# Issuing the value products of a pair of heads as one alternating group in batch 0 of a fused attention and two-MLP kernel

## The chip, the cores and the metric

The kernel runs on one core of one Trainium2 chip, alone. The metric is the time of one execution on the device, in microseconds (us), the median of several executions. The engines of a core are named as the profile names them: PE (TensorE, matmuls; PEld is its weight loads), DVE (VectorE), ACT (ScalarE), POOL (GpSimd) and SP (the queue that issues most DMAs).

## The reference, cut to what matters

Three stages follow one another: attention, a token-shift MLP with a gate, and a mixer MLP. The change lies in the attention, batch 0.

```python
k_sum = k.reshape(B, H, nb, block, D).max(axis=3)      # B, H, S, D = 2, 8, 768, 64; block 32, nb 24
v_sum = v.reshape(B, H, nb, block, D).mean(axis=3)
scores_l = where(|i - j| < 16, scale * q @ k.T, -1e9)  # a band around the diagonal
scores_s = scale * q @ k_sum.T + log(block)            # the block summaries
a = softmax(concat([scores_l, scores_s]))
x = a @ concat([v, v_sum])                             # -> x: (B, S, H * D)
...
xk = mu_k * x + (1 - mu_k) * x_prev                    # second stage: 512 -> 1024 -> 512
k = relu(xk @ w_k); v = k * k @ w_v; r = sigmoid(xr @ w_r); x = r * v
...                                                    # third stage: token mixing, then 512 -> 1536 -> 512
```

## The kernel before

**Attention.** Each batch has 6 tiles of 128 tokens (t = 0 to 5) and 4 pairs of heads; e = 0 or 1 is the head within a pair. Of one e, the four heads are handled together. For a tile and an e, `s_stage` writes scores (tile sp; 120 columns: 24 block summaries and 96 keys) by 8 matmuls on PE, then for each head one DVE instruction takes mask and minimum (L385, out to pe) and one ACT instruction the exponential with its row sum (L387). `t_stage` transposes the four pe on PE (tile pt) and copies them to SBUF (tile PT, three buffers) on DVE (L410) or ACT (L408). `v_stage` multiplies PT with the values: 8 matmuls of 120x64 by 64 columns for an e, into the lower (e = 0) or upper (e = 1) 64 partitions of tile pv. When both halves of pv are there, batch 0 adds the reciprocal of the row sums: they are turned (L436, L437), spread over partitions by 8 matmuls (tile rb, in one of the two buffers of pt), ACT copies pv to xT (L444), and DVE multiplies by rb (L445). xT is the input of the second stage.

**Steps.** In batch 0 a step is one (t, e): 12 steps, with a filler matmul (spin) in the first eight. In batch 1 a step is a tile with both e: there the 16 value matmuls of a tile are issued as one group that alternates between e = 1 and e = 0, kept in that order by `in_line`; the row sums are applied earlier, on POOL (L399). `LAGS = 1, 2` says how many steps after its scores a tile is transposed and multiplied. In batch 0 before, each e has its own value group of 8.

**Work put in between.** `main()` is the second stage, in chunks of 256 tokens: `mixed` makes xk on POOL (tmp, L533), DVE (xk, L534; xl, L536) and ACT; then for each of four g come 24 matmuls to ko and, one g later, 12 to acc (L544). `attention()` yields costs, and `main()` is advanced by a credit of them. `weights.step()` prepares one of 16 weights of 128x512 in this stage: ACT (L153), two DVE passes (L157, L163, through tile wf with two buffers), a rounding copy on ACT (L174) and the rest on POOL (L175). Chunk 0 goes through all 16. For batch 1, DVE also makes block maxima (ks, L287) and block sums (vrs, L309), and POOL puts the maxima into kw (L293) before its scores can start.

**Order.** A scheduler sets the order of each engine's instructions from program order, given priorities and its own times; after that each engine runs its list in order and waits on semaphores. So a change to when a group is emitted can move instructions on every engine.

Of the kernel before, what the change touches and what calls it, by code (L numbers as in the profile page):

```python
# [23 lines left out]
LAGS = 1, 2  # L24
# [33 lines left out]
def fused_kernel(ctx, tc, q, k, v, vt, mu, w_k, w_v, w_r, w_t1, w_t2, w_c1, w_c2, out):  # L58
# [230 lines left out]
    @ahead(HK)  # L289
    def kw_sums(b, t):  # L290
        st = state[b]
        for o in (0, WC - NB):
            nc.gpsimd.tensor_scalar(st["kw"][t][:, :, o:o + NB], st["ks"], 1.0, 1.0, ALU.mult, ALU.mult)  # L293
# [10 lines left out]
    @ahead(HR)  # L304
    def vt_sum(b, j):
        st = state[b]
        if j == 0:
            st["vr"] = at.tile([128, NP, NB], F32, tag="vrs", bufs=1, name="vrs")
        r = nc.vector.tensor_reduce(st["vr"][:, 2 * j:2 * j + 2], st.pop(("vt", j)), AX.X, ALU.add)  # L309
        if b == 0:  # L310
            behind(r, lows[-1:])

    @ahead(HR)
    def v_gather(b):
        st = state[b]
        vp = bank("pt", 2, [128, NP, 128], "vp")
        for p in range(NP):
            nc.tensor.transpose(vp[:NB, p], st["vr"][:, p], ident)
        st["vs"] = at.tile([NB, DM], F32, tag="vs", bufs=1, name="vs")
        nc.scalar.activation(st["vs"], vp[:NB].rearrange("p g e -> p (g e)"), AF.Copy, scale=1.0 / BLOCK)  # L320

    @ahead(HL)
    def vw_load(b, t):
        ws = []
        for half in range(2):
            w = ybuf[:NC, 2 * t + half] if b == 0 else at.tile([NC, DM], F32, tag="vw", bufs=VB, name="vw")
            row, srow = (NB, 0) if half == 0 else (0, NK)
            key = 128 * t + 64 * half
            after(nc.sync.dma_start(w[row:row + NK], v[b, key:key + NK]))
            ws.append((w, srow))  # L330
        st_of(b)["vw"][t] = ws

    def vw_sums(b, t):
        ahead(HV if b or t == 0 else 0)(copy_sums)(b, t)
# [12 lines left out]
    @ahead(HL)  # L347
    def q_load(b, t):
        if b == 0:
            st_of(b)["qT"][t] = xT[:, :, XB + 1 + 128 * t:XB + 129 + 128 * t]  # L350
        else:
            st_of(b)["qT"][t] = at.tile([128, NP, 128], F32, tag="qT", bufs=QB, name="qT")
        after(nc.sync.dma_start(st_of(b)["qT"][t], q[b, t]))
# [93 lines left out]
    done_tiles = [0]  # L447

    def attention():
        slots = {}  # L450
        n0 = 2 * NT
        steps = [(0, t, (e,)) for t in range(NT) for e in range(2)] + [(b, t, (0, 1)) for b in range(1, B) for t in range(NT)]
        for i in range(len(steps) + 1):
            if i < len(steps):
                b, t, es = steps[i]
                if b and t == 0:
                    yield from prep(b)
                zs = s_stage(b, t, es)
                if len(es) == 1:
                    for what, z, lag in zip((t_stage, v_stage), (zs[0], zs), LAGS):  # L460
                        slots.setdefault(min(i + lag, n0), []).append(((i + lag, lag), what, z))
                else:
                    slots[i + 1] = [((i, 1), n_stage, z) for z in zs] + [((i, 2), t_stage, z) for z in zs] + [((i, 3), v_stage, zs)]
                if i < SPIN_UNITS:
                    spin(SPIN)
                yield 0.95 * len(es)
                if es[-1] == 1 and t + 1 < NT:
                    kw_sums(b, t + 1)
                if b and t == 0:
                    vw_sums(b, 0)  # L470
                if i in VSUM:
                    vt_sum(0, VSUM.index(i))
                if i == VSUM[1]:
                    v_gather(0)
                    vw_sums(0, 0)
            for _, what, z in sorted(slots.get(i, ()), key=lambda s: s[0]):
                what(z)
                if what is t_stage:
                    yield 0.43
                elif what is v_stage:  # L480
                    yield 0.7 * len(z)
                    done_tiles[0] += len(z) / 2
            if i < len(steps):
                if 0 in es:
                    if t + 1 < NT and t + 1 not in state[b]["vw"]:
                        vw_load(b, t + 1)
                    if b and t + 2 < NT:
                        q_load(b, t + 2)
                if i == VSUM[1]:
                    vw_sums(0, 1)  # L490
                elif 1 in es and t + 1 < NT and i > VSUM[1]:
                    vw_sums(b, t + 1)
                if b + 1 < B:
                    for e in es:
                        prep_next(b + 1, 2 * t + e)

    def prep_next(b, j):

        if j >= 4 and j % 2 == 0:
            k_load(b, j // 2 - 2)  # L500
        if j == 9:
            vt_load(b, 0)
            q_load(b, 0)
        if j == 10:
            vt_load(b, 1)
        if j == 2 * NT - 1:
            for t in (4, 5):
                k_load(b, t)
            vw_load(b, 0)
            q_load(b, 1)  # L510

    def prep(b):

        for t in range(NT):
            k_max(b, t)
            yield HOLD / (NT + 2)
        for j in range(2):
            vt_sum(b, j)
            yield HOLD / (NT + 2)
        kw_sums(b, 0)  # L520
        v_gather(b)
# [97 lines left out]
    def spin(n):  # L619

        o = bank("ko", 1, [128, 4, 128], "spin")
        for _ in range(n):
            after(nc.tensor.matmul(o, ident, ident.unsqueeze(1).to_broadcast([128, 4, 128]), start=True, stop=True))
# [50 lines left out]
    for n, cost in enumerate(attention()):  # L674
        weights.pin = PIN0 if n < N0 else PIN1
        if n >= W0 and n % SIDE_EVERY == 0:
            weights.step()
        credit += cost * (RATIO if n < NR else RATIO2)
        while credit > 0:
            got = next(hidden, None)  # L680
            if got is None:
                credit = 0.0
                break
            credit -= got
# [458 lines left out]
```

## Time and profile before

| | |
|---|---|
| time, median of 3 (lowest to highest) | 502.85 us (502.44 to 504.47) |
| span of the profiled execution, first to last instruction | 502.8 us |
| its granted PE clock, mean | 0.990 |
| PE busy | 487.9 us, 97% |
| DVE, ACT, POOL busy | 316.6, 250.9, 217.4 us |

The profile has one execution; its own time is its span, 502.8 us, which equals the median. Times in it are us from its first instruction. Batch 0 of the attention lies between 12 and 75 us. In the rows of a timeline two records of PE belong to one matmul here ("x16" is 8 matmuls).

### The profile page before, as it was taken

To read this page: it belongs to the slowest core of one execution; us is meant where nothing else is said; L and a number is where in the kernel's file an instruction comes from. 1 tells how busy PE (TensorE), PEld (TensorE's weight loads), DVE (VectorE), ACT (ScalarE), POOL (GpSimd) and SP (SyncE) were. 2 spreads that over 40 slices of the span, in tenths; PEclk is the share of its full clock that TensorE was granted. 3 is DMA by queue.
4 is the path that set the end of the run, shared out by engine and by line. 5 is a ranking of instruction groups with operands and counts; after the bars stand their busy time and mean duration, and the time that the engine had idled before them with its cause. 6 is when DMAs were issued, how large, how long until landed. Compare 5 with 4: busy or idle time off the path is not lost.

```text
span 502.8 us, 8800 instructions
## 1 busy us (share of the span) xinstructions
PE 487.9 (97%) x3278; PEld 407.1 (81%) x3278; DVE 316.6 (63%) x638; ACT 250.9 (50%) x569; POOL 217.4 (43%) x266
## 2 busy tenths in 40 slices
PE   7999997999999999999999998999999999999996
PEld 3567785888888888888888887878898999989995
DVE  2888998641514355598889789646579638354352
ACT  1778746862544555686585455454554435111110
POOL 6335587862441447345516434774942813000000
PEclk9899998899999999999999999999999999999999
DMA  8999930221000650000551998639351405253102
GB/s 264 323 309 361 335 87 14 88 80 40 20 1 2 224 196 0 1 0 14 161 163 21 400 394 313 211 112 316 117 168 42 142 31 164 52 200 117 52 1 83
DMA packets 35914, 70.63 MB, mean 140 GB/s; under 512 B 3072, under 2 KB 12288, under 8 KB 35872
## 3 DMA queue, kind: packets, MB, share of 16 engines
q1 hardware_dynamic: 34288, 69.09, 42.0%
q10 hardware_dynamic: 1584, 0.98, 0.7%
q8 instruction: 26, 0.43, 0.3%
q14 instruction: 16, 0.13, 0.1%
HBM read 60.04 MB, written 9.44 MB: 138 GB/s over the span
## 4 chain that ended last, share of the span: by engine, by line
PE 75%; DMA 10%; DVE 8%; POOL 2%; ACT 2%; issue 1%; SPq 1%; DVEq 0%; POOLq 0%
PE ko L544 13%; PE acc L544 13%; PE o L955 12%; PE m L544 11%; PE o L983 7%; PE ro L544 7%; PE go L544 5%; DMA wst<-in_moe_w_k_dram 3%; DMA xT<-in_q_dram 3%; DMA ybuf<-in_v_dram 2%; DVE wf L163 2%; PE pv L425 2%; PE sp L367 2%; PE h L544 2%; DMA wst<-in_moe_w_ch_dram 1%
## 5 line engine op out<-in xcount | busy, mean ns | idle before, releaser
L175 POOL TENSOR_TENSOR w<-wf,w 128x512 fp32r<-128x512 f32 x50 | 69.1, 1387 | 77.3 <-ACT w L174 72.4
L544 PE MATMUL ko<-xh,w 128*128 128x256 f32 x384 | 76.3, 288 | 1.7 <-POOL w L175 0.9
L544 PE MATMUL m<-u,w 128*128 128x256 f32 x504 | 65.1, 283 | 0.8 <-DVE mw L846 0.7
L544 PEld LDWEIGHTS m<-u,w 128*128 128x128 f32 x504 | 63.4, 191 | 2.9 <-DVE mw L846 0.9
L544 PEld LDWEIGHTS ko<-xh,w 128*128 128x128 f32 x384 | 61.1, 188 | 5.4 <-POOL w L175 1.1
L544 PE MATMUL acc<-w,kh 128*128 128x512 f32 x192 | 61.7, 404 | 0.0
L955 PE MATMUL o<-w,gh 128*128 128x512 f32 x192 | 59.1, 391 | 0.0
L544 PE MATMUL ko<-xl,w 128*128 128x256 f32 x192 | 54.4, 283 | 1.1 <-DVE xl L536 1.1
L559 POOL TENSOR_TENSOR kl<-rl,kh 128x512 fp32r<-128x512 f32 x24 | 33.7, 1405 | 44.6 <-ACT kh L558 36.4
L163 DVE SCALAR_TENSOR_TENSOR wf<-wst,wf 128x512 int32<-128x512 int32 x50 | 47.6, 956 | 8.2 <-ACT wst L153 7.1
L174 ACT CAST w<-wf 128x512 fp32r<-128x512 f32 x50 | 30.9, 620 | 42.8 <-DVE wf L163 40.9
L557 DVE TENSOR_TENSOR rl<-rl 128x512 f32<-128x512 f32 x24 | 19.6, 819 | 48.4 <-ACT rl L556 48.2
L387 ACT ACTIVATE pe<-pe,mn 128x120 f32<-128x120 f32 x96 | 36.6, 383 | 14.6 <-DVE mn L385 14.3
L153 ACT ACTIVATE wst<-wst 128x512 f32<-128x512 f32 x62 | 41.1, 675 | 2.1 <-DMA wst<-in_moe_w_ch_dram 2.1
L544 PEld LDWEIGHTS acc<-w,kh 128*128 128x128 f32 x192 | 35.3, 192 | 7.3 <-ACT pe L387 0.3
L955 PEld LDWEIGHTS o<-w,gh 128*128 128x128 f32 x192 | 34.7, 188 | 6.2
L534 DVE SCALAR_TENSOR_TENSOR xk<-xT,mus,tmp 128x256 f32<-128x256 f32 x52 | 36.5, 733 | 4.1 <-POOL tmp L533 3.2
L544 PEld LDWEIGHTS ko<-xl,w 128*128 128x128 f32 x192 | 36.2, 188 | 2.1 <-DVE xl L536 1.3
L544 PE MATMUL acc<-w,kl 128*128 128x512 f32 x96 | 37.7, 403 | 0.0
L955 PE MATMUL o<-w,gl 128*128 128x512 f32 x96 | 37.1, 391 | 0.0
L544 PE MATMUL go<-u,w 128*128 128x512 f32 x144 | 35.6, 393 | 0.0
L784 ACT ACTIVATE gh<-m 128x512 fp32r<-128x512 f32 x24 | 14.2, 596 | 42.7 <-DVE m L846 42.7
(120 smaller groups left out, 964.5 us busy)
## 6 DMA issues: line engine op xcount, KB each, us to landing
wst<-in_moe_w_ch_dram SPq DMA_DIRECT2D x36, 512.0 KB, 6.9
w<-stored SPq DMA_DIRECT2D x24, 512.0 KB, 4.9
stored<-w SPq DMA_DIRECT2D x24, 256.0 KB, 4.7
wst<-in_moe_w_k_dram SPq DMA_DIRECT2D x8, 512.0 KB, 7.4
wst<-in_moe_w_v_dram SPq DMA_DIRECT2D x8, 512.0 KB, 9.5
wst<-in_moe_w_tok_dram SPq DMA_DIRECT2D x6, 512.0 KB, 4.7
out_dram<-o SPq DMA_DIRECT2D x12, 256.0 KB, 2.4
kw<-in_k_dram SPq DMA_DIRECT2D x9, 320.0 KB, 5.1
```

Source lines behind the costliest of these rows:

```text
L153: a = nc.scalar.activation(top.bitcast(F32), top.bitcast(F32), AF.Prelu, scale=2.0 ** -112, alpha=2.0 ** 32)
L163: nc.vector.scalar_tensor_tensor(wi, top, 3, wi, ALU.logical_shift_left, ALU.bitwise_or)
L174: r = nc.scalar.copy(hi, src)
L175: eng.tensor_tensor(lo, src, hi.bitcast(F32), ALU.subtract)
L387: nc.scalar.activation(pe, pe, AF.Exp, bias=mn[:, p:p + 1], scale=-1.0, accum_out=den[:, p:p + 1])
L534: nc.vector.scalar_tensor_tensor(xk[:, d], xT[:, d, x0:x0 + MW], mu[:, d:d + 1], tmp, ALU.mult, ALU.add)
L544: nc.tensor.matmul(o, l, r, start=(first and i == 0), stop=(last and i == 3 * n - 1))
L557: nc.vector.tensor_tensor(rl, rl, rl, ALU.mult)
L559: nc.gpsimd.tensor_tensor(lo, rl, hi.bitcast(F32), ALU.subtract)
L784: nc.scalar.activation(hi, o, AF.Relu)
L955: nc.tensor.matmul(accs[c][t], l, r, start=(first and j == 0 and i == 0), stop=(last and j == 1 and i == 2))
L983: nc.tensor.matmul(accs[0][t], l, r, start=(k == 0 and i == 0), stop=(k == NF2 - 1 and i == 2))
```

## The change

`v_stage` is called once a tile in batch 0, at the lag of e = 1, with both heads of each pair, and so issues its 16 matmuls in the alternating order of batch 1. The transposes stay where they were, one e at a time.

```diff
     def attention():
-        slots = {}
+        slots, pair = {}, []
         n0 = 2 * NT
...
                 zs = s_stage(b, t, es)
                 if len(es) == 1:
-                    for what, z, lag in zip((t_stage, v_stage), (zs[0], zs), LAGS):
-                        slots.setdefault(min(i + lag, n0), []).append(((i + lag, lag), what, z))
+                    pair.extend(zs)
+                    slots.setdefault(min(i + LAGS[0], n0), []).append(((i + LAGS[0], LAGS[0]), t_stage, zs[0]))
+                    if es[0] == 1:
+                        slots.setdefault(min(i + LAGS[1], n0), []).append(((i + LAGS[1], LAGS[1]), v_stage, list(pair)))
+                        pair.clear()
                 else:
```

Lines behind the change have a number higher by 3 in the changed program (L544 is L547 there).

On PE, tile 3 of batch 0. Before, from the scores sp_1000 (tile 4) to the normalisation rb_873: PT_689 is e = 0, PT_776 e = 1.

```order
L367 MATMUL sp_1000<-kw_107,xT_84 64x120 x8
L425 MATMUL pv_781<-PT_689,ybuf_71 64x64 x8
L405 MATMUL pt_850<-ident_61,pe_737 120x128
L405 MATMUL pt_850<-ident_61,pe_740 120x128
L405 MATMUL pt_850<-ident_61,pe_743 120x128
L405 MATMUL pt_850<-ident_61,pe_746 120x128
L425 MATMUL pv_781<-PT_776,ybuf_71 64x64 x8
L441 MATMUL rb_873<-ident_61,dens_521 64x128 x8
```

The same place in the changed program, up to the third of the 16 value matmuls (the next 13 go on alternating, and rb_864 follows them); PT_671 is e = 0, PT_776 e = 1.

```order
L367 MATMUL sp_968<-kw_107,xT_84 64x120 x3
L405 MATMUL pt_810<-ident_61,pe_737 120x128
L405 MATMUL pt_810<-ident_61,pe_740 120x128
L405 MATMUL pt_810<-ident_61,pe_743 120x128
L405 MATMUL pt_810<-ident_61,pe_746 120x128
L425 MATMUL pv_845<-PT_776,ybuf_71 64x64
L425 MATMUL pv_845<-PT_671,ybuf_71 64x64
L425 MATMUL pv_845<-PT_776,ybuf_71 64x64
```

The transposes no longer stand between the two halves; they are ahead of all 16, and the first value matmul now needs the PT of e = 1.

On DVE, from the block sums (vrs) of the second half of batch 1 to the first masking of batch 1's tile 0 (L385, printed as ISA). Before:

```order
L309 TENSOR_REDUCE vrs<-ybuf 128x48
L163 SCALAR_TENSOR_TENSOR wf<-wst,wf 128x512
L157 TENSOR_SCALAR wf<-wst 128x512
L163 SCALAR_TENSOR_TENSOR wf<-wst,wf 128x512
L445 TENSOR_TENSOR xT<-xT,rb 128x4x128
L157 TENSOR_SCALAR wf<-wst 128x512
L534 SCALAR_TENSOR_TENSOR xk<-xT,mus,tmp 128x256
L163 SCALAR_TENSOR_TENSOR wf<-wst,wf 128x512
L534 SCALAR_TENSOR_TENSOR xk<-xT,mus,tmp 128x256
L557 TENSOR_TENSOR rl<-rl 128x512
L157 TENSOR_SCALAR wf<-wst 128x512
L385 ISA pe,mn<-sp,mask_182 128x120
```

In the changed program:

```order
L309 TENSOR_REDUCE vrs<-ybuf 128x48
L560 TENSOR_TENSOR rl<-rl 128x512
L410 COPY PT<-pt 120x512
L163 SCALAR_TENSOR_TENSOR wf<-wst,wf 128x512
L157 TENSOR_SCALAR wf<-wst 128x512
L385 ISA pe,mn<-sp,mask_182 128x120
L385 ISA mn 128x1
```

The first L163 in each is that of the twelfth weight. The masking of batch 1 has moved up to directly behind it, and the last xT of batch 0 and the xk that come from it have moved behind the masking.

On DVE, from the first xl to the copy of PT for tile 4, e = 1. Before:

```order
L536 TENSOR_TENSOR xl<-xk,xh 128x1024
L437 RECIPROCAL dens<-dens 128x8
L157 TENSOR_SCALAR wf<-wst 128x512
L445 TENSOR_TENSOR xT<-xT,rb 128x4x128
L410 COPY PT<-pt 120x512
```

In the changed program:

```order
L539 TENSOR_TENSOR xl<-xk,xh 128x1024
L163 SCALAR_TENSOR_TENSOR wf<-wst,wf 128x512
L157 TENSOR_SCALAR wf<-wst 128x512
L163 SCALAR_TENSOR_TENSOR wf<-wst,wf 128x512
L436 TENSOR_SCALAR dens<-dens 128x8
L437 RECIPROCAL dens<-dens 128x8
L445 TENSOR_TENSOR xT<-xT,rb 128x4x128
L287 TENSOR_REDUCE ks<-kw 128x4x4 x2
L157 TENSOR_SCALAR wf<-wst 128x512
L287 TENSOR_REDUCE ks<-kw 128x4x4
L537 SCALAR_TENSOR_TENSOR xk<-xT,mus,tmp 128x256
L410 COPY PT<-pt 120x512
```

The copy on which tile 4's value group now waits has more instructions ahead of it after xl.

## Rows read from the trace of the kernel before

**Rows 1.** The page: busy us of each engine (share of the span) and instructions.

```profile
PE 487.9 (97%) x3278; PEld 407.1 (81%) x3278; DVE 316.6 (63%) x638; ACT 250.9 (50%) x569; POOL 217.4 (43%) x266
```

**Rows 2.** Busy time by stretch: us, PE, PEld, DVE, ACT, POOL (instructions), PEclk, DMA, GB/s.

```profile
40.00:70.00 30.00, 27.88 (x296) 23.27 (x293) 30.00 (x75) 20.83 (x57) 18.88 (x19) 1.00 0.94 308
...
80.00:90.00 10.00, 7.23 (x50) 5.30 (x51) 9.82 (x36) 6.84 (x24) 7.03 (x9) 0.70 0.14 36
...
200.00:503.00 303.00, 296.67 (x1617) 254.77 (x1615) 196.89 (x283) 135.71 (x242) 112.03 (x88) 1.00 0.40 136
```

**Rows 3.** Timeline of PE, tile 1 of batch 0: start, length, instruction [idle before <- releaser].

```profile
34.39 1.15 PE L425 MATMUL pv<-PT,ybuf 120*64 120x64 f32 x16
35.46 0.33 PE L405 MATMUL pt<-ident,pe 128*120 128x128 f32 x1
35.72 0.33 PE L425 MATMUL pv<-PT,ybuf 120*64 120x64 f32 x2
```

**Rows 4.** Timeline of PE, a tile of batch 1, both heads alternating.

```profile
100.39 1.15 PE L425 MATMUL pv<-PT,vw 120*64 120x64 f32 x32
```

**Rows 5.** Timeline of DVE around its one wait for PE after 35 us.

```profile
37.05 0.19 DVE L437 RECIPROCAL dens<-dens 128x8 f32<-128x8 f32 x1
39.04 0.69 DVE L445 TENSOR_TENSOR xT<-xT,rb 128x512 f32<-128x512 f32 x1 [1.79 <-PE rb L441]
```

**Rows 6.** Timeline of PE, 80 to 94 us: its waits, and two score groups.

```profile
80.32 0.39 PE L544 MATMUL ko<-xh,w 128*128 128x256 f32 x1 [0.74 <-ACT rl L556]
...
81.75 0.50 PE L544 MATMUL ko<-xh,w 128*128 128x256 f32 x2 [0.93 <-POOL w L175]
...
84.71 0.63 PE L367 MATMUL sp<-kw,qT 64*64 64x120 f32 x2 [1.52 <-issue]
...
87.28 1.87 PE L367 MATMUL sp<-kw,qT 64*64 64x120 f32 x30
...
93.05 1.04 PE L367 MATMUL sp<-kw,qT 64*64 64x120 f32 x30
```

**Rows 7.** Busy time by stretch of 2 us, columns as in rows 2.

```profile
84.00:86.00 2.00, 1.29 (x4) 0.91 (x5) 2.00 (x16) 2.00 (x10) 2.00 (x3) 0.50 0.10 25
...
90.00:92.00 2.00, 2.00 (x9) 1.59 (x9) 1.54 (x13) 2.00 (x12) 2.00 (x4) 0.81 0.89 273
```

**Rows 8.** Timeline of DVE, 76 to 88 us.

```profile
76.26 1.51 DVE L157 TENSOR_SCALAR wf<-wst 128x512 int32<-128x512 int32 x1 [1.18 <-POOL w L175]
...
78.48 0.68 DVE L445 TENSOR_TENSOR xT<-xT,rb 128x512 f32<-128x512 f32 x1
...
79.88 0.69 DVE L534 SCALAR_TENSOR_TENSOR xk<-xT,mus,tmp 128x256 f32<-128x256 f32 x1 [0.38 <-POOL tmp L533]
...
82.17 0.69 DVE L534 SCALAR_TENSOR_TENSOR xk<-xT,mus,tmp 128x256 f32<-128x256 f32 x1
...
83.73 0.27 DVE L385 CUSTOM_DVE_ANT_0 pe<-sp,mask 128x120 f32<-128x120 f32 x1
...
85.35 1.87 DVE L534 SCALAR_TENSOR_TENSOR xk<-xT,mus,tmp 128x256 f32<-128x256 f32 x2
```

**Rows 9.** Timeline of POOL, 79 to 93 us.

```profile
79.34 0.96 POOL L533 TENSOR_SCALAR tmp<-xT,oms 128x256 f32<-128x256 f32 x2 [1.85 <-DVE xT L445]
80.27 1.42 POOL L175 TENSOR_TENSOR w<-wf,w 128x512 fp32r<-128x512 f32 x1
81.68 0.91 POOL L533 TENSOR_SCALAR tmp<-xT,oms 128x256 f32<-128x256 f32 x1
...
89.14 1.38 POOL L399 TENSOR_SCALAR pe<-pe,den 128x120 f32<-128x120 f32 x4 [2.60 <-DVE den L396]
90.49 2.52 POOL L175 TENSOR_TENSOR w<-wf,w 128x512 fp32r<-128x512 f32 x2
```

**Rows 10.** Timeline of DVE, two successive instructions at tile 4's normalisation.

```profile
54.17 0.67 DVE L445 TENSOR_TENSOR xT<-xT,rb 128x512 f32<-128x512 f32 x1
54.77 0.68 DVE L410 COPY PT<-pt 120x512 f32<-120x512 f32 x1
```

## Prediction, made before the changed kernel was run

> **What bounds the kernel now.** I read three things in this order: the busy shares, the stretches, then the timelines of PE and DVE. PE is busy 487.9 of 502.8 us [rows 1], and from 200 us to the end it is busy 296.67 of 303 at full clock [rows 2]. So whatever PE is behind or ahead by at the end of the attention is carried to the end of the kernel. The time can only change through what PE does, or waits for, before that. The lost time lies early: between 40 and 70 us DVE is busy 30.00 of 30, PE 27.88; between 80 and 90 us DVE is busy 9.82 of 10, PE only 7.23, at a mean granted clock of 0.70 [rows 2]. From 39 to 89 us DVE is the engine that is full. Besides the attention it prepares 16 weights, and PE's work in between needs them one after the other.
>
> In 80 to 92 us PE shows what that costs: waits of 0.74, 0.93 and 1.52 us, 3.2 us in all, and then score matmuls at 1.87 us for a group that takes 1.04 us five us later [rows 6]. The granted clock is 0.50 at 84 to 86 and 0.81 over 90 to 92 [rows 7], that is 1.2 GHz of 2.4 until about 91. PE had been idle for more than a third of 84 to 86. The 0.81 is what 90 to 92 gives if the clock is at half until 90.8; so some 6.8 us at half clock, less the 0.7 that PE was idle in 84 to 86, cost half of 6.1, about 3.1 us. The wait of 1.52 us is put down to "issue", but the place tells what it is: scores of batch 1's tile 1 need a score buffer that the masking of tile 0 has read, and DVE comes to that masking only at 83.73 [rows 8].
>
> **What the change removes.** One head of each pair, 8 value matmuls, takes PE from 34.39 to 35.46, 1.07 us [rows 3]. In batch 1 the 16 matmuls of a tile, alternating, show the same length of 1.15 us as the 8 there do [rows 3, 4]: the two heads write different halves of the partitions and run beside each other. So a tile of batch 0 should fall from 2.14 to 1.07 us, and six tiles give back 6.4 us of PE. No instruction and no DMA is added or taken away.
>
> One rule of the Trainium skill bears on the price. In tile 1 transposes and value matmuls take turns, and there a transpose alone holds PE 0.26 us, from 35.46 to 35.72 [rows 3]. TensorEngine Tiling (Array Packing), section Key Properties, says that changing the tiling mode, not just the tile, drains the engine. The trace agrees: turns cost more there than matmuls of one kind in a row. By that rule the change would also give back two changes of mode a tile, and in tile 1, where the changed order still has four turns, none. I add nothing for it.
>
> **Why 6.4 us is not the answer.** A PE that is done sooner gains only if its next work is there. Up to 39 us DVE waited for PE once worth naming, 1.79 us for rb at tile 1 [rows 5]. Eight matmuls fewer would give 1.07 of it; but rb also needs the reciprocal that starts at 37.05 and takes 0.19 [rows 5], and it starts little later than that now. I take 0.5, with bounds 0 and 1.07. From there to 76 us DVE has no wait for PE, so what PE saves in tiles 2 to 5 buys nothing by itself: it becomes waiting for DVE. It is put at nothing, and its cover is DVE's full list; if DVE were not full, it would be worth up to 4 x 1.07 = 4.3.
>
> **What the new order does.** The scheduler has redone the lists. Up to the second DVE pass (L163) of weight 12, the two DVE lists hold the same instructions, in another order. Behind it they differ in a way that matters (the second place shown above). Counting the lists up to each weight's second pass, the changed one has, up to weight 13, four score-mask steps more (0.2 us each, from the starts 83.73 to 85.35 for eight [rows 8]); up to weight 14, eight such steps more, and one xk and the last xT less; up to weight 15, four xk and that xT less, against one short instruction more; up to weight 16, two xk less and three short ones more. So the masking of batch 1's tile 0 comes directly after weight 12, around 76 to 78 us instead of 83.7, and PE's wait of 1.52 us has no cause any more. Weight 15 comes earlier by the xk of 0.69, 0.69 and 1.87 (two) and the xT of 0.68 [rows 8], 3.9 us; with the 0.5 from above 4.4 us on DVE. The xk that are put off feed chunk 2, far behind.
>
> PE must have weight 15 complete, POOL's part too. Before, POOL ends weight 13 at 81.69 and weight 15 at about 91.75, with 2.60 us of waiting for the softmax sums in between [rows 9]. That is 10.1 us. In its changed list POOL has between these two: eight normalisations (2 x 1.38), four tmp, weight 14, one kl (which I price like weight 14) and weight 15. With 1.42 twice, 1.26 for weight 15, and two tmp of 0.48 and two of 0.91 [rows 9] that is 9.6 us; with four of 0.91 it is 10.5. Weight 13 itself comes about 0.9 earlier: the 1.18 us wait at 76.26 [rows 8] falls away because POOL now does weight 11 before kl, four mask steps cost 0.8, and the 0.5 is added. POOL so gives weight 15 a lead of 0.9 - 0.4 = 0.5 us, or 1.4 with the cheaper tmp, if its list is full all the way. The lead lies between 0.5 (POOL's count at its dearest) and 4.4 (DVE's). I take 3.3, nearer to DVE's, because DVE is the full one in that stretch (9.82 of 10) and POOL has slack (7.03) [rows 2].
>
> Can PE use it? From 80 to 92 us it has 3.2 us of waits and loses 3.1 to the half clock, 6.3 together, so 3.3 fits in. What PE has done when weight 15's matmuls end is about equal: the changed order has put the values of batch 1's tile 0 ahead (1.07 us) and left the scores of tile 2 behind (1.04 us [rows 6]). The sum: 502.8 - 3.3 = **499.5 us**; the execution's 502.8 is also the median, so nothing is converted. With the lead between 0.5 and 4.4 this case alone gives 498.4 to 502.3.
>
> **The rivals.** *Hidden.* DVE is full, so its 16 weights end when they did, and the order only changes who waits; only the 0.5 remains: 502.3. For it: equal instructions up to weight 12. Against it: the lists are not equal at weight 15.
>
> *All of it shows.* PE's waits and its slow stretch both vanish, and all 6.4 us of PE appear: 496.4. The clock could add 3.1: 493.3. For it: PE would have scores, transposes and values to do in 78 to 90 us. Against it: POOL's count.
>
> *A new wait, and the clock with it: slower.* Both heads' PT must now be there before the first value matmul. At tile 4 that of e = 1 is copied on DVE, before at 54.77, 0.6 after the xT ahead of it [rows 10]; in the changed list eleven instructions stand between xl and that copy, where three did (the third place shown above): two more L163, three ks, one xk, one L157, one L436. At 0.6 each (0.1 for the short L436) the eight cost 4.3, less 0.6 because one of them stood ahead of xl before: the copy comes at most 3.7 later, 3.2 with the 0.5 from tile 1. PE fills a part of that with the ko matmuls that it has; I price the wait at 2 us. If PE's idling there brings the clock down as at 84 us, another 3.1 us go, and with a lead of only 0.5 left: 502.8 + 2 + 3.1 - 0.5 = 507.4. It decides from where the granted clock falls to 0.5 between 45 and 75 us. TensorE: Matmul & The Clock Gate, The HAM clock gate, says that the throttled state is the default and activity releases it; rows 7 agree, the fall comes after PE had been idle in part. Against it: PE at 27.88 of 30 in 40 to 70 kept 1.00 [rows 2]; I expect some 24 there, still busy four fifths.
>
> That the change doesn't alternate after all is excluded: the order shown above does.
>
> **How the numbers follow.** Chances: my forecast 0.47, hidden 0.26, all of it 0.14, slower 0.13. The bound for a change that can be told from none is 0.5%, 2.5 us: 500.3 and 505.4. Of the forecast's own range (498.4 to 502.3) the part above 500.3 lies within 0.5%; since I take a lead near its upper end, that is about 0.14 of the 0.47. Faster: 0.33 + 0.14 = 0.47; same: 0.14 + 0.26 = 0.40; slower 0.13. The range 495.5 to 504.5 holds the forecast, hidden, and the part of "all of it" without a change of clock, and leaves out the slower case and the largest gain, some 0.2.
>
> **What would show it.** Right: value groups of 32 records in about 1.1 us in batch 0 (six of them, 1.07 less each); DVE full between 40 and 76 as before, and PE less busy there; the first masking of batch 1 before 80 us; no wait of PE for scores near 84 us; weight 15 off POOL near 88 to 90; PE behind its 96th ko matmul 3 us earlier than before, and that distance kept to the end. Wrong: a fall of the granted clock before 75 us; DVE waiting for row sums or score buffers between 40 and 80; a lead at 95 us that is gone by 200 us.

## The result, and the profile after

The changed kernel takes 510.28 us (median of 4, 508.65 to 518.17), the kernel before 503.66 beside it. The ratio is 1.0132, interval 1.0103 to 1.0160: slower, where faster was forecast, and outside the range. Ratios here leave disturbed executions out; medians are over all. The profiled execution took 510.11 us; its span is 508.3, 5.5 more than before.

The page, busy us of each engine, against [rows 1]:

```profile
PE 490.0 (96%) x3278; PEld 406.2 (80%) x3278; DVE 319.6 (63%) x638; ACT 251.0 (49%) x569; POOL 213.3 (42%) x266
```

The work on PE became less and its busy time more. By stretches, columns as in [rows 2]:

```profile
40.00:70.00 30.00, 25.34 (x251) 21.42 (x248) 29.86 (x66) 19.67 (x56) 15.35 (x16) 0.77 0.92 297
80.00:90.00 10.00, 8.93 (x61) 5.33 (x60) 7.15 (x15) 6.26 (x19) 7.04 (x13) 1.00 0.19 59
200.00:503.00 303.00, 299.03 (x1631) 256.77 (x1630) 197.55 (x284) 137.29 (x245) 112.04 (x90) 1.00 0.39 133
```

From 40 to 70 us the granted clock is 0.77, before it was 1.00, and PE is less busy, with DVE as full as before. From 80 to 90 it is the other way round: 1.00, before 0.70. The timeline of PE at tiles 2 to 5 of batch 0 (start, length, instruction, idle before it):

```profile
40.54 1.97 PE L425 MATMUL pv<-PT,ybuf 120*64 120x64 f32 x32
47.37 1.11 PE L405 MATMUL pt<-ident,pe 128*120 128x128 f32 x4 [1.48 <-DVE xT L445]
48.40 1.98 PE L425 MATMUL pv<-PT,ybuf 120*64 120x64 f32 x32
...
58.65 1.98 PE L425 MATMUL pv<-PT,ybuf 120*64 120x64 f32 x32 [2.90 <-issue]
...
75.67 1.15 PE L425 MATMUL pv<-PT,ybuf 120*64 120x64 f32 x32
```

The groups alternate as meant: 32 records in 1.15 us where the granted clock is full, 1.97 where it is at half (0.50 in 48 to 50 and 58 to 60 us). Tile 4's waits 2.90 us; what it waits for stands in the timeline of DVE, which also has the row of tile 1's normalisation, batch 1's first masking, and the second pass of weight 15:

```profile
36.22 0.63 DVE L445 TENSOR_TENSOR xT<-xT,rb 128x512 f32<-128x512 f32 x1
...
57.87 0.68 DVE L410 COPY PT<-pt 120x512 f32<-120x512 f32 x1
...
76.15 0.28 DVE L385 CUSTOM_DVE_ANT_0 pe<-sp,mask 128x120 f32<-128x120 f32 x1
...
82.00 0.69 DVE L163 SCALAR_TENSOR_TENSOR wf<-wst,wf 128x512 int32<-128x512 int32 x1
```

All this looks like the slower rival come true. The experiments say otherwise. More places matter for them. The timeline of POOL from the end of weight 13 (79.95) over weight 14 (85.24) to weights 15 and 16:

```profile
82.96 1.40 POOL L399 TENSOR_SCALAR pe<-pe,den 128x120 f32<-128x120 f32 x4 [3.01 <-DVE den L397]
84.34 0.94 POOL L536 TENSOR_SCALAR tmp<-xT,oms 128x256 f32<-128x256 f32 x2
85.24 1.44 POOL L175 TENSOR_TENSOR w<-wf,w 128x512 fp32r<-128x512 f32 x1
86.66 2.35 POOL L399 TENSOR_SCALAR pe<-pe,den 128x120 f32<-128x120 f32 x4
88.99 0.48 POOL L536 TENSOR_SCALAR tmp<-xT,oms 128x256 f32<-128x256 f32 x1
89.43 1.26 POOL L562 TENSOR_TENSOR kl<-rl,kh 128x512 fp32r<-128x512 f32 x1
90.68 0.65 POOL L536 TENSOR_SCALAR tmp<-xT,oms 128x256 f32<-128x256 f32 x1
91.29 2.52 POOL L175 TENSOR_TENSOR w<-wf,w 128x512 fp32r<-128x512 f32 x2
```

POOL first waits 3.01 us for the row sums (den) of batch 1. Weight 15 leaves it at 92.55 (half of the last row), before at 91.75 [rows 9]: later, not earlier. And kl, which stands behind all this in POOL's list, is ready at 90.69. PE waits for it:

```profile
90.75 0.74 PE L547 MATMUL acc<-w,kl 128*128 128x512 f32 x2 [1.36 <-POOL kl L562]
```

This is the last wait of any size on PE before 230 us. In the kernel before, the last one is that of the scores at 84.71 [rows 6].

The timeline of PE in batch 1, scores (sp) and transposes (pt):

```profile
96.78 0.63 PE L367 MATMUL sp<-kw,qT 64*64 64x120 f32 x12
97.33 0.33 PE L405 MATMUL pt<-ident,pe 128*120 128x128 f32 x1
97.59 0.42 PE L367 MATMUL sp<-kw,qT 64*64 64x120 f32 x2
97.94 0.33 PE L405 MATMUL pt<-ident,pe 128*120 128x128 f32 x1
98.19 0.42 PE L367 MATMUL sp<-kw,qT 64*64 64x120 f32 x4
98.55 0.32 PE L405 MATMUL pt<-ident,pe 128*120 128x128 f32 x1
98.80 0.42 PE L367 MATMUL sp<-kw,qT 64*64 64x120 f32 x2
99.14 0.33 PE L405 MATMUL pt<-ident,pe 128*120 128x128 f32 x1
99.40 0.42 PE L367 MATMUL sp<-kw,qT 64*64 64x120 f32 x4
99.76 0.33 PE L405 MATMUL pt<-ident,pe 128*120 128x128 f32 x1
100.01 0.42 PE L367 MATMUL sp<-kw,qT 64*64 64x120 f32 x4
100.36 0.33 PE L405 MATMUL pt<-ident,pe 128*120 128x128 f32 x1
100.45 0.37 PE L547 MATMUL ko<-xh,w 128*128 128x256 f32 x1
100.65 0.28 PE L405 MATMUL pt<-ident,pe 128*120 128x128 f32 x1
100.68 0.36 PE L547 MATMUL ko<-xl,w 128*128 128x256 f32 x1
```

PE never waits here, yet 16 scores and 6 transposes hold it from 96.78 to 100.45. And three waits of PE in the gate of the second stage (ro) and behind it (ho); the trace of before has none between 200 and 300 us (PE busy 100.00 of 100 there):

```profile
242.45 0.73 PE L547 MATMUL ro<-w,xh 128*128 128x512 f32 x2 [0.59 <-ACT xh L538]
277.98 0.74 PE L547 MATMUL ro<-w,xh 128*128 128x512 f32 x2 [0.51 <-DVE ybuf L718]
281.87 1.65 PE L547 MATMUL ho<-h,w 128*128 128x512 f32 x6 [0.83 <-DVE ybuf L718]
```

### The profile page after: what moved, and what is told of

Its sections match the earlier page's. It is cut to its first block, busy times and chain, and to the rows that moved or that the text cites. A ratio compares the mean times of both kernels' runs of the same rounds, so it can differ in the third digit from the quotient of the medians.

```text
span 508.3 us, 8794 instructions
## 1 busy us (share of the span) xinstructions
PE 490.0 (96%) x3278; PEld 406.2 (80%) x3278; DVE 319.6 (63%) x638; ACT 251.0 (49%) x569; POOL 213.3 (42%) x266
## 4 chain that ended last, share of the span: by engine, by line
PE 57%; DVE 19%; DMA 10%; ACT 7%; issue 3%; POOL 1%; SPq 0%; DVEq 0%; ACTq 0%; POOLq 0%
PE o L958 12%; PE m L547 11%; PE ko L547 8%; PE acc L547 8%; PE o L986 6%; PE go L547 5%; DVE wf L163 5%; DMA wst<-in_moe_w_k_dram 3%; DMA xT<-in_q_dram 3%; DVE wf L157 3%; DVE xk L537 3%; DMA ybuf<-in_v_dram 2%; PE sp L367 2%; ACT wst L153 2%; DVE rl L560 1%
## 5 line engine op out<-in xcount | busy, mean ns | idle before, releaser
L175 POOL TENSOR_TENSOR w<-wf,w 128x512 fp32r<-128x512 f32 x50 | 67.1, 1347 | 74.5 <-ACT w L174 68.6
L547 PE MATMUL ko<-xh,w 128*128 128x256 f32 x384 | 77.0, 287 | 0.1
L547 PE MATMUL m<-u,w 128*128 128x256 f32 x504 | 65.1, 283 | 0.7 <-DVE mw L849 0.7
L547 PEld LDWEIGHTS m<-u,w 128*128 128x128 f32 x504 | 63.4, 190 | 2.9 <-DVE mw L849 0.9
L547 PEld LDWEIGHTS ko<-xh,w 128*128 128x128 f32 x384 | 61.5, 189 | 2.8 <-issue 1.1
L547 PE MATMUL acc<-w,kh 128*128 128x512 f32 x192 | 62.1, 408 | 0.0
L547 PE MATMUL ko<-xl,w 128*128 128x256 f32 x192 | 54.7, 285 | 0.0
L163 DVE SCALAR_TENSOR_TENSOR wf<-wst,wf 128x512 int32<-128x512 int32 x50 | 47.5, 956 | 10.9 <-ACT wst L153 9.7
L547 PEld LDWEIGHTS acc<-w,kh 128*128 128x128 f32 x192 | 34.8, 190 | 8.5 <-issue 1.2
L547 PE MATMUL acc<-w,kl 128*128 128x512 f32 x96 | 37.8, 403 | 1.5 <-POOL kl L562 1.5
L547 PEld LDWEIGHTS ko<-xl,w 128*128 128x128 f32 x192 | 36.2, 189 | 0.9
L547 PE MATMUL go<-u,w 128*128 128x512 f32 x144 | 35.9, 394 | 0.0
```

The lines of the kernel that those rows point to most:

```text
L163: nc.vector.scalar_tensor_tensor(wi, top, 3, wi, ALU.logical_shift_left, ALU.bitwise_or)
L175: eng.tensor_tensor(lo, src, hi.bitcast(F32), ALU.subtract)
L547: nc.tensor.matmul(o, l, r, start=(first and i == 0), stop=(last and i == 3 * n - 1))
```

## The experiments

Four theories. **A**: the late value group waits for the second PT, PE idles, its clock falls. **B**: the alternation doesn't pay in batch 0. **C**: the lists that the scheduler made around the groups cost the time (a list is the order of one engine's instructions). **D**: a side effect of the edit: `attention()` yields six times less, which sets another pace for weights and second stage. A fifth, **E**, came later: within C, the turns that PE takes between differently shaped matmuls. Times are medians; the ratio is to the kernel before, run beside each. "Turns" are counted in PE's list: changes between scores, values or normalisations, and the rest (transposes, second stage, fillers), from batch 1's first score on (or the 72nd ko matmul, if that is earlier).

| kernel | us | ratio [95%] | turns |
|---|---|---|---|
| before | 503 to 504 | 1 | 52 |
| changed | 510.28 | 1.0132 [1.0103, 1.0160] | 72 |
| e1_late_plain | 511.25 | 1.0164 [1.0131, 1.0197] | 66 |
| e2_pt_act | 508.70 | 1.0101 [1.0081, 1.0121] | 57 |
| e3_spin | 509.95 | 1.0142 [1.0102, 1.0182] | 50 |
| e4_tiles01 | 502.65 | 0.9988 [0.9965, 1.0011] | 48 |
| f1_turn | 507.58 | 1.0098 [1.0082, 1.0113] | 59 |
| c4_before_turn | 500.79 | 0.9957 [0.9941, 0.9972] | 40 |
| c1_before_pt_act | 502.28 | 1.0001 [0.9975, 1.0027] | 59 |
| e8_pace | 507.84 | 1.0100 [1.0075, 1.0126] | 72 |
| f2_turn_pace | 508.22 | 1.0117 [1.0078, 1.0156] | 69 |
| f3_turn_tiles01 | 500.61 | 0.9957 [0.9932, 0.9981] | 40 |
| f4_turn_tiles0145 | 498.98 | 0.9912 [0.9898, 0.9927] | 38 |
| g1_fill | 498.79 | 0.9912 [0.9897, 0.9927] | 43 |
| h1_before_order | 502.22 | 0.9965 [0.9947, 0.9983] | 52 |
| h2_fill_at_waits | 510.61 | 1.0131 [1.0101, 1.0161] | 72 |
| h3_fill_order | 498.86 | 0.9899 [0.9870, 0.9929] | 43 |
| h4_turn_pt_act | 500.54 | 0.9929 [0.9895, 0.9964] | 43 |
| i1_after_gather | 504.68 | 1.0034 [1.0016, 1.0052] | 26 |
| i2_best_gather | 495.76 | 0.9824 [0.9777, 0.9872] | 26 |

### One thing changed in the new kernel

**No alternation, same late place.**

```diff
-        for p in range(NP):
-            for half in range(2):
-                for z in zs[::-1]:
+        for p, half, z in ([(p, half, z) for z in zs for p in range(NP) for half in range(2)] if b == 0 else
+                           [(p, half, z) for p in range(NP) for half in range(2) for z in zs[::-1]]):
...
```

> The changed kernel, but the 16 value matmuls of a tile of batch 0 run as 8 of e = 0 and then 8 of e = 1, at the late place, without taking turns. Theory A (the late group waits for a PT that the full DVE copies late, PE idles, the granted clock falls): the eight of e = 0 can start without that PT, so PE idles less at tiles 2 to 4, but each tile takes 2.14 us of PE at full clock again; clock in 40 to 60 above the changed kernel's 0.76, time between 503 and 510. Theory B (taking turns does not pay in batch 0): the time falls back to the 503.7 of before. Theory C (it is the scheduler's new order elsewhere, not the wait): time stays near 510, clock near 0.76.

511.25. B is out: the time does not fall back. The windows of this run show more:

```profile
40.00:70.00 30.00, 26.49 (x282) 22.32 (x280) 30.00 (x69) 20.83 (x58) 17.73 (x18) 1.00 0.94 306
```

The clock of 40 to 70 is back at 1.00 and the kernel is as slow as ever. That is the first blow to A, although PE has more value work here; C's clock, near 0.76, was missed too.

**All PT copies on ACT; more fillers; two tiles only.**

```diff
-PT_ACT = ((0, 0), (1, 0), (1, 1))
+PT_ACT = ((0, 0), (0, 1), (1, 0), (1, 1))     # e2
-SPIN, SPIN_UNITS = 1, 8
+SPIN, SPIN_UNITS = 1, 12                      # e3
-                    if es[0] == 1:
+                    if es[0] == 1 or not (t < 2):   # e4
```

> The changed kernel, with the copy of PT of e = 1 in batch 0 on ACT too, so that the value groups wait for nothing on DVE. Theory A: the waits at tiles 2 to 4 go, the granted clock in 40 to 60 comes back to 0.95 or more, time 503 or less. Theory B: clock back, time still above 506. Theory C: the copies are not the cause; the time moves by up to 5 us either way and without a tie to the clock at 40 to 60.

508.70. Tile 4's wait for the copy is gone, yet PE idles 8.3 us in 40 to 70 at a clock of 0.78: it waits for other things, most of them on DVE (busy 28.45 of 30). Taking one wait away hands PE the next.

> The changed kernel, with the filler matmul in the first 12 steps in place of 8. Theory A: four more fillers (about 0.5 us of PE each) fall into PE's idle time at tiles 4 and 5; the clock at 56 to 64 stays at 1.00, the fall at 40 to 50 remains; time 507 to 509. Theory B: 510 to 512, as only work is added. Theory C: moves by several us without a tie to the clock.

509.95: no gain beyond the interval. Its one profile differs from its own median by 6 us, so I read no times from it.

> The change made for tiles 0 and 1 alone; tiles 2 to 5 are issued as before. Theory A: these two tiles have no wait for a late PT, so clock and waits are those of before and 2.1 us of PE go, of which at most 0.5 shows: 501.5 to 503.7. Theory B: 504 to 506, a third of the loss. Theory C: anything between 500 and 508, by what order the scheduler finds.

502.65, not told from before, which A had expected as well. PE's three waits of [rows 6] are there too (0.61, 0.92 and 1.52 us, the last at 83.00). The loss comes with tiles 2 to 5.

### Turns, pace, and a control without value groups

`in_turn` keeps scores and transposes of batch 1 in program order among themselves on PE (f1 on the changed kernel, c4 on the one before). e8 yields 0.7 at the old place of the first head and 0.7 at the group.

```diff
+    def in_turn(inst):
+        behind(inst, turn[-1:])
+        turn.append(inst)
...
                     if len(es) > 1:
                         in_line(m)
+                        in_turn(m)
...
-            nc.tensor.transpose(pt[:NC, p], z["P"][p], ident)
+            m = nc.tensor.transpose(pt[:NC, p], z["P"][p], ident)
+            if z["u"][0]:
+                in_turn(m)
```

> The changed kernel, with the scores and the transposes of batch 1 kept in program order among themselves on PE, so that a score matmul and a transpose no longer take turns there. Between 12 and 190 us the changed kernel spends 23.98 us on scores and 13.40 on transposes, before 21.33 and 12.46: 3.6 us more for the same matmuls. Theory C (the new order of batch 1 costs): scores and transposes fall back to about the figures of before in 90 to 190 us, time 506.5 to 508. Theory A (waits at tiles 2 to 4 of batch 0 and the clock alone): nothing in 40 to 70 changes, time 509.5 to 510.5.

> The kernel before with the same rule for scores and transposes of batch 1, as a control: it takes few turns there already, so both theories expect 501.5 to 504. If it moves by more than 2.5 us, the rule does something of its own, and the run beside it can't be read as a test of the turns alone.

> The kernel before, values still in two groups of 8, with the copy of PT of e = 1 on ACT. No value group is late here. Theory A: DVE loses six copies of 0.68 us in its full stretch, so the time falls or stays: 500 to 503.7. Theory C: this edit too makes the scheduler put batch 1's scores late (behind the 216th and 264th ko matmul, before behind the 96th and 144th), and the time goes up as in the changed kernel: 506 to 509.

> The changed kernel, with the cost of a value group yielded twice as before (0.7 at the old place of the first head, 0.7 at the group), so that the second stage and the weights are emitted at the places in the program that they had before. Theory D (the six missing yields set another pace for weights and second stage, and this costs the time): 503 to 505. Theories A and C: 508 to 511, since groups and order of batch 1 stay as in the changed kernel.

f1 507.58 and c4 500.79: the rule is worth 2 to 3 us on either kernel, c4 lying below what either theory allowed. So it does not tell them apart, but suggests that turns have a price. c1 502.28: it too puts batch 1's scores late, and loses nothing, which was A's forecast; lateness alone is not C. e8 507.84: between A/C and D, and its interval overlaps that of the changed kernel; from 200 to 300 us its PE is busy 100.00, the three waits of the gate are gone, and they were 1.9 us. The pace is at most a part, not the whole.

### Both together, tiles, and fillers

f2 is f1 and e8 together; f3 and f4 make the change in it for some tiles only. g1 adds fillers to f2, which the value group then overwrites:

```diff
         line.clear()
+        if b == 0 and t in (2, 3, 4):
+            for _ in range(3):
+                in_line(nc.tensor.matmul(pv, ident, ident.unsqueeze(1).to_broadcast([128, 4, 128]), start=True, stop=True))
```

> The changed kernel with the rule on turns in batch 1 and the pace of before, together. Alone they took 2.7 and 2.4 us off the changed kernel's 510.3. If the two are separate: about 505. Theory A says that what is then left against the kernel before with the same rule (500.8) is the waits and the half clock of 40 to 70 us: PE waits of 2.9 (value group of tile 4) and about 3 us (transposes behind the last normalisation's buffer) still there, granted clock in 40 to 70 below 0.93, time 504 to 506. If turns and pace are the whole loss: 500 to 502.

> The rule on turns, the pace of before, and the change for tiles 0 and 1 alone. Without the rule these two tiles gained 0.9 us; the rule alone on the kernel before gives 500.8. Both theories expect 499.5 to 500.8, faster than either kernel.

> The rule on turns, the pace of before, and the change for tiles 0, 1, 4 and 5, with tiles 2 and 3 in two groups as before. Theory A, if the wait at tile 4's group (2.9 us) is what costs: 503 to 505, the wait and a half clock at 56 to 64 still there. Theory A, if the late groups of tiles 2 and 3 set it off by putting the normalisation's buffer in the transposes' way: 499 to 501.5, no half clock in 40 to 70.

> The changed kernel with the rule on turns and the pace of before, and three filler matmuls of 512 columns (about 0.5 us each at full clock) on PE ahead of the value groups of tiles 2, 3 and 4, into the bank that the group then overwrites. They are 4.5 us of useless work, put where PE waits. If the half clock is a good part of the loss: the granted clock in 40 to 70 comes back to 0.95 or more and the time falls below that of the same kernel without fillers (about 505) by 1 to 3 us. If the waits cost and the clock does not: the clock comes back, and the time stays or goes up by as much as the fillers stand on the path (up to 4.5).

f2 508.22: the two gains do not add, and all three forecasts (500 to 502, 504 to 506, about 505) are missed. The scores fall from 9.86 to 6.81 us of PE between 90 and 200, but the scheduler now mixes the values with second-stage matmuls, and they go from 7.30 to 10.38. f3 500.61 is where both theories had it. f4 498.98 fits the second reading of A (499 to 501.5), which blames the late groups of tiles 2 and 3; the change in tiles 4 and 5 loses nothing by itself. g1 498.79: 9.4 us less than f2, with the clock at 1.00, and with more useless work than I had thought (three fillers took 2.84 us, not 1.5). By this run alone A would look proven: clock and time are what it asked for. But the fillers also changed every list.

### Lists pinned: the test of A against C

Each engine's instructions are recorded as they are issued, and then chained in a list taken from another build, so that the scheduler has no choice. No run pins a kernel to its own lists and changes nothing else; h2 comes nearest, with fillers added to the lists of the changed kernel. The edit, with arguments cut:

```diff
+    for n, seq in json.loads(zlib.decompress(base64.b85decode(ORDER))).items():
+        mine = nc.log[n]
+        for a, b in zip(seq, seq[1:]):
+            tc.add_manual_dep(mine[b].ins, mine[a].ins.name, ...)
```

> The change without the scheduler: every engine runs the list of the kernel before, pinned instruction by instruction, and on PE alone the eight value matmuls of e = 0 of each batch 0 tile are moved to those of e = 1 and alternate with them. If the late group itself costs (it waits for the second PT, PE idles, the clock falls): 506 or more. If the loss lies in the lists that the scheduler made around the groups: 499 to 503, with the granted clock of 40 to 70 at 0.95 or more, and six groups of about 1.1 us.

> The changed kernel with its own lists pinned on every engine, and seven filler matmuls of 512 columns on PE at its waits alone: one ahead of the scores before tile 2's value group, three ahead of the transposes before tile 3's, three ahead of tile 4's. A filler took 0.95 us in the run with fillers, so 6.7 us of useless work into some 5.5 us of waits. If the half clock after the waits is a good part of the loss: the granted clock of 40 to 70, 0.68, 0.84 and 0.79 by tens, comes back to 0.95 or more, and the time falls to 504 to 508. If the waits cost and the clock does not: clock back, time 509.5 to 512.

> The lists of the run with fillers (498.8), pinned on every engine, with the nine fillers left out: 8 us of useless PE work less. If the fillers help because they keep the clock up: the granted clock falls in 40 to 70 and the time goes up, to 501 or more. If they help because the scheduler, seeing PE busy, made other lists: 496 to 499, with the clock at 0.95 or more.

h1, the change in the lists of before (and with the pace of e8): 502.22, 0.9965, a little faster. The groups themselves cost nothing. h2, the lists of the changed kernel with its waits filled: in the windows by tens

```profile
40.00:50.00 10.00, 10.00 (x140) 7.13 (x141) 10.00 (x39) 10.00 (x38) 5.22 (x5) 1.00 1.03 388
50.00:60.00 10.00, 8.41 (x80) 6.06 (x77) 9.86 (x16) 5.16 (x12) 4.17 (x6) 1.00 1.09 333
60.00:70.00 10.00, 8.49 (x65) 6.84 (x62) 10.00 (x13) 4.56 (x8) 5.99 (x6) 1.00 0.72 181
```

the clock is full throughout, 0.999 over the profiled span, and in its timeline of PE tile 4's group waits 0.28 us in place of 2.90, at the same place in time:

```profile
55.92 2.74 PE L164 MATMUL pv<-ident 128*128 128x512 f32 x6
58.94 1.15 PE L164 MATMUL pv<-PT,ybuf 120*64 120x64 f32 x32 [0.28 <-DVE PT L164]
```

The time is 510.61, unchanged; the profiled execution is the fastest of five, 508.20, against 508.65 for the fastest of the changed kernel. The fillers put useless work in the place of the waits, so that this run speaks of the clock and not of the waits. But further on PE meets the wait from above again, at nearly the same time (90.75 there):

```profile
91.04 0.74 PE L164 MATMUL acc<-w,kl 128*128 128x512 f32 x2 [1.35 <-POOL kl L164]
```

What PE won or lost on the way is gone there. h3, the lists of g1 without its fillers, in 40 to 70 us:

```profile
40.00:70.00 30.00, 22.80 (x253) 19.11 (x253) 29.24 (x78) 22.13 (x60) 21.15 (x25) 0.89 0.87 289
```

PE idles 7.2 us there and the clock falls to 0.89, and the time is 498.86, that of g1. So A is refuted as the cause: in the lists of the changed kernel a full clock brings no gain, and in those of g1 waits and a low clock bring no loss. In 40 to 70 us DVE is full (30.00, 29.86, 29.24 in h1, h2, h3), and what PE does in its slack, and how fast, does not show in the time. C stands: with the same groups, the lists of before give 502.22 and those of the changed kernel 510.28.

> No value groups: the kernel before with the rule on turns in batch 1 (500.8 alone) and all PT copies on ACT (502.3 alone, batch 1's scores late). A candidate for the fastest: if the two add up, 499.5 to 500.5; if the copies matter to DVE's full stretch once the turns are gone, 498 to 499.5.

h4 500.54: they do not add up beyond c4's 500.79, as far as the intervals tell.

### What in the lists: the turns

The count of turns alone does not order the table: kernels with 50 to 59 turns take 502.2 to 510.0 us, and i1 and i2, both with 26, lie 8.9 us apart. What the turns cost within one set of lists can be tested. i1 and i2 put each of batch 1's six score groups and six value groups at the place of its first matmul and leave all else in the lists as it was (i1 in those of the changed kernel, i2 in those of h3; only PE's list differs from that of h2 and h3, the four others are the same). In outline, as it is done on PE's list before the kernel is built:

```python
for j in ORDER["tensor"]:
    new += [j] if j not in group else members[group[j]] if j == members[group[j]][0] else []
```

> The changed kernel with its own lists pinned on every engine, except that on PE each of batch 1's six score groups and six value groups, which the lists split and mix with other matmuls, is gathered at the place of its first matmul. In the lists PE changes behind batch 0 between scores, values or normalisations, and the 128-row matmuls (transposes and second stage) 72 times in the changed kernel, 52 before; gathered 26 times. Nothing in 40 to 70 us changes. Theory E (these turns cost, about 0.2 us each by the rows in which a score matmul and a transpose alternate at 0.61 us a pair): 46 turns fewer, 6 to 9 us less, 501 to 504.5. Theories A and C without the turns: 509 to 511.

> The same gathering on the lists of the filler run without its fillers (498.9), where PE takes 43 such turns behind batch 0; gathered 26. Theory E: 17 turns fewer at 0.2 us, 495 to 496.5, the fastest of all. Without it: 498 to 500.

i1 504.68, 5.6 us less than the changed kernel and just above the 501 to 504.5 forecast, and i2 495.76, 3.1 less than h3 and the fastest of all (0.9824). PE in i1, the tile from above:

```profile
98.60 1.05 PE L164 MATMUL sp<-kw,qT 64*64 64x120 f32 x32
99.59 0.87 PE L164 MATMUL pt<-ident,pe 128*120 128x128 f32 x6
100.21 0.37 PE L164 MATMUL ko<-xh,w 128*128 128x256 f32 x1
```

The 16 scores and 6 transposes take 1.61 us (98.60 to 100.21), in the changed kernel 3.67: 2.06 us for ten turns more, 0.2 each. All scores of batch 1 from 90 to 200 us on PE (stretch, length, busy, clock, DMA), in the kernel before, the changed one and i1:

```profile
90.00:200.00 110.00, 7.35 (x128) 1.00 0.22 73
```

```profile
90.00:200.00 110.00, 9.86 (x128) 0.98 0.21 69
```

```profile
90.00:200.00 110.00, 4.21 (x128) 0.97 0.21 69
```

The same 128 records, and 5.65 us between the last two, about the gain of i1. (The records overlap their neighbours a little, so this is no exact sum; and i1's PE waits 5.2 us in 70 to 100, the changed kernel's 1.9, so a part of what is freed becomes waiting.) From its last wait to the end of the last acc matmul, i1's PE needs 165.2 us, the changed kernel's 171.3.

So it is shown that the turns in the changed kernel cost it some 5.6 us. It is not shown that they are the whole difference to the kernel before, and the rows say that they are not: by them the kernel before pays 3.1 us for turns too, which leaves 2.5 for the change. And i1, with half the turns of the kernel before, is still a little slower (1.0034): other things in the lists cost the rest.

The Trainium skill, TensorEngine Tiling (Array Packing), section Key Properties, says that a change of the tiling mode drains the engine. These traces agree where a 64*64 score matmul meets a 128-row transpose (the 0.2 us from above); that it is a drain, and not another latency, no run here shows.

## Why the prediction was wrong, step by step

**What bounds the kernel: right at the end, not quite in 70 to 90.** What PE is behind at the end of the attention is carried to the end. The last acc matmul (second stage) ends at 262.01, before at 256.78, 5.2 of the span's 5.5 us later; from it to the last matmul of the kernel it takes 242.30 us, before 241.95. But DVE was not "the engine that is full" all the way "From 39 to 89": in the trace of before, it is busy 8.34 of 10 us in 70 to 80, and its longest wait there is for POOL (1.18 [rows 8]).

**6.4 us of work removed: right in size.** Groups of 32 records in 1.15 us at full clock; h1 has them with the lists of before.

**"What PE saves in tiles 2 to 5 buys nothing": right**, and more so than I argued: h2 puts 6.6 us of fillers (1.02, 2.84 and 2.74) on PE there, and its time stays.

**0.5 us up to 39: too small.** Tile 1's normalisation on DVE comes at 36.22 without a wait, 2.8 us earlier than before [rows 5]. By tile 4's copy nothing of it is left (57.87 against 54.77 [rows 10]), as DVE's list has more ahead of it.

**The new order: half right.** Masking of batch 1 at 76.15 (76 to 78 forecast); the 1.52 us wait near 84 gone; the clock of 80 to 90 at 1.00; weight 15's second pass on DVE 5.1 us earlier (82.00, before 87.14), where I had worked out 4.4.

**The term that failed: the lead of 3.3 us at weight 15.** Its bounds were 0.5 to 4.4; it came out at -0.8 (POOL 92.55 against 91.75). From weight 13's end to weight 15's POOL took 10.1 us before, I counted 9.6 to 10.5, and it took 12.6 (79.95 to 92.55). The work was priced right: without its wait of 3.01 us at 82.96, POOL took 9.59. (Four normalisations took 2.35 us instead of 1.38, but the tmp and the kl took less than priced.) What failed is the condition "if its list is full all the way". The 10.1 us of before held a wait of 2.60 us for softmax sums; in the changed list I put that wait at nothing, and it came as 3.01. The masking of batch 1 had moved up, its normalisation stood ahead of weight 14 on POOL, and the last step of the row sums (den, L397) came on DVE only at 82.61. I took a lead near DVE's count because DVE was full and POOL had slack; from 80 to 90 us DVE is now busy 7.15 of 10. And PE did not wait for weight 15 at all, but for the kl that stands behind the same wait in POOL's list (90.75).

**The step that was missing: PE's own list behind weight 15.** I compared the lists of DVE and POOL, and PE's only at tile 3, and took "the lead is kept to the end" from PE being busy. A busy PE can be busy with turns. I had the price in [rows 3], 0.26 us for a transpose between value matmuls, and had even weighed the rule, but for batch 0 alone, where the change removes turns. In batch 1 the new list has 20 more.

The time as it came out, up to the end of the last acc matmul, 5.2 us later than before: PE's last wait before 230 us (leaving out a few hundredths) ends 6.0 us later (90.75 for kl, before 84.71 for scores), and from there PE takes 0.8 us less (171.3 against 172.1). So the 1.52 us wait that I took away was replaced by one that ends later. Within the second part the turns weigh on the changed kernel: its scores between 90 and 200 us take 2.5 us more (9.86 against 7.35), and the wait of ro at 242.45 adds 0.6; against that it has 32 score records fewer left and less time at half clock (PEclk 1.00 and 0.83 in 80 to 90 and 90 to 100, before 0.70 and 0.96). What turns cost i1 shows. The wait for kl is read from one execution of each kernel and tested by no run alone; e8, h2 and i1 have it too (1.36, 1.35 and 1.21 us). It does not set the time by itself: h3, 11 us faster, waits for kl at 91.68, but has only 159.6 us of PE left by then. How much of the second stage the list lets PE do ahead of that wait counts as much, and which place in the lists decides this stays open. Open too are e8, whose 2.4 us I can't divide between its clock of 1.00 in 90 to 100, the waits of the gate, and chance, and c1: with 59 turns it takes 502.3, and has PE idle for only 0.2 us in 70 to 100.

**The rivals.** "A new wait, and the clock with it" gave 507.4, the nearest time, and all its signs came: tile 4's wait 2.90 (2 priced), half clock in 40 to 70. It was given 0.13. It is right on what is seen there and wrong on the cause, so its time was met by luck. "Hidden", 502.3, is near what the change does if nothing else moves: h1, 502.22. Missing from the list was the rival that the scheduler's new lists cost more than the change is worth.

**The signs.** I had named "a fall of the granted clock before 75 us" as proof of a wrong forecast. It was true and told nothing of why. Another sign, "DVE waiting for row sums", came near the cause: row sums were waited for, but by POOL.

## What to carry to other kernels

Where a scheduler makes the lists, an edit is two changes: what it does, and what the scheduler does around it. Here the first was worth -1.6 us and the second +8; pin the lists of before to measure the first alone. Price a changed list on the engine that bounds the kernel, to its end, turns between tile shapes included. When counting a lead on another engine, keep the waits that its list had, unless the new order removes their cause. And an idle stretch or a low clock costs only if its engine is the one waited for: fill it and look at the time before calling it the cause.

## What was not expected of the hardware

Between a 64*64 score matmul and a 128-row transpose PE loses about 0.2 us each way here, with no wait in the trace: it reads as busy. Between transposes and second-stage matmuls it loses little: in the rows above two ko and a transpose take 0.43 us from 100.45 (the next starts at 100.88), about 0.1 more than such matmuls do in a row.

The mean granted clock over the span told little of the time. The changed kernel took 510.11, 510.46 and 508.65 us at 0.983, 0.989 and 0.992; with fillers (h2) one execution took 508.20 at 0.999 and four 509.86 to 511.55 at 0.995. Much of the half clock that h2 removed lay where DVE was full.
